# Delta-rule attention with an MLP: transposes in 128x128 blocks, one Gram matmul for K and Q, and a scheduler that models instruction fetch

## The chip, the cores and the metric

The kernel runs on one core of a Trainium2 chip. The metric is the device time of one execution in microseconds (us). A run over 1.5% above the fastest of its kernel counts as slow. All ratios and the medians of the experiments are of fast runs alone; all profiles are of fast runs. TensorE is called PE in the profile, its weight loads PEld (each matmul first loads its stationary operand); VectorE is DVE, ScalarE ACT, GpSimd POOL. An engine waits for another by a semaphore, a counter that the other one raises.

## The reference, cut to what matters

```python
# q, k, v: (4, 8, 768, 48); beta: (4, 8, 768)
k_n = k / (np.linalg.norm(k, axis=-1, keepdims=True) + 1e-06)
for t in range(S):
    y[:, :, t] = q_t @ state
    v_old = state^T @ k_n_t
    state = state + beta_t * outer(k_n_t, v_t - v_old)
# then, on x = y with heads joined: (3072, 384)
h = x @ w_in                 # 384 -> 2048
out = gelu_tanh(h) @ w_out   # 2048 -> 384
```

The recurrence is done in 12 chunks of 64 tokens for 32 heads (16 pairs). Within a chunk a 64x64 triangular system is solved for every head, by a Newton iteration on small matmuls. Only the state passes from chunk to chunk. The MLP runs on tiles of one or two finished chunks, so its matmuls can be laid between the small ones of later chunks.

## The kernel before: the parts that matter

The program is built as a list of some 1040 operations. A list scheduler in the kernel file orders them, with modelled durations, a table of priorities found by search (`OFFSET`), and a tolerance for waiting (`NEAR`). An operation on TensorE is a batch of matmuls. The file has no model of how instructions reach an engine.

```python
UNITS = [[0]] + [[c, c + 1] for c in range(1, NCH - 1, 2)] + [[NCH - 1]]

# Gram: K K^T and K Q^T of a chunk, separately; 4 quadrants of the array, 64 columns each
for o in range(2):
    def gd(h=h, o=o):
        for m in range(p0 // 2, p1 // 2):
            for (hh, a) in ((0, 0), (1, 1), (0, 1), (1, 0)):
                ...
                r.append((bank(h, hh)[cc, mo:mo + C], KQT[i][rr, 0, m, cc], KQT[i][rr, o, m, cc], True, True, True))
    # ... (cut: one DVE multiply of 1024 columns for W, one for DT)

# transposes of W for the Newton iteration: every 64x64 block, to both row halves
def tr_w(t):
    for p in range(n):
        for o in range(2):
            for a in range(2):
                ins = t.transpose(xb(o)[rows(a ^ o), p, :], W[rows(a), p, :], identB[rows(a), :])
```

## Time and profile before

| | before |
|---|---|
| median of 3 runs | 327.86 us (326.28 to 331.25, the last one slow) |
| profiled span | 324.9 us |
| matmuls, each with a weight load | 7998 |
| TensorE, VectorE, ScalarE, GpSimd busy | 76%, 53%, 52%, 37% |
| instruction packets | 63 |

From the page of the kernel before: busy time and number of instructions of each engine, and one of the DMA queues (packets, MB, share of the 16 DMA engines):

```profile
span 324.9 us, 16859 instructions
PE 247.8 (76%) x7998; PEld 163.1 (50%) x7998; DVE 173.7 (53%) x227; ACT 169.8 (52%) x255; POOL 120.3 (37%) x80
...
q8 instruction: 63, 1.03, 1.3%
```

63 packets of 16 KB: 1.03 MB. Matmuls and weight loads are 15,996 instructions, and 15,996 / 256 = 62.5. So this queue carries TensorE's program, 256 instructions to a packet. Such a packet is called a block below, and the place where one ends and the next begins a border.

From the table of waits of the kernel before (who waited for what: us in total, times, longest):

```profile
PEld ps L342 <- issue: 58.8, 80, 3.9
...
PE ps L342 <- issue: 35.4, 34, 3.4
```

"issue" is a wait for nothing that the profile shows. PE and PEld overlap, so the two rows count many of the same gaps twice; they are not to be read as 94 us of lost time.

From the chain of waits of the kernel before, 195 to 225 us (start, length, what):

```profile
196.24 0.91 issue
197.16 2.98 PE ps L342 x103
200.14 0.57 issue
200.71 3.28 PE ps L342 x115
203.99 3.38 issue
207.37 8.33 PE ps L342 x215
...
218.76 0.66 issue
219.42 3.75 PE ps L342 x128
223.17 0.90 issue
```

The reader should see a rhythm: about 120 matmuls (some 250 instructions), a gap without a releaser, and again. Counted in TensorE's own instruction order, the gaps lie exactly 256 apart.

From the groups of instructions of the kernel before, the two that the change rewrites (busy us, mean ns, idle before):

```profile
L342 PE MATMUL ps<-KQT 48*64 48x64 bf16 x768 | 13.5, 215 | 5.3 <-issue 2.7 <-ACT KQT L335 1.1 <-DMA KQT<-KQ 1.0
...
L687 PE MATMUL ps<-identB,Wi 64*64 64x64 bf16 x768 | 11.8, 210 | 10.4 <-issue 7.3 <-DVE Wi L326 2.0 <-DVE F_0 L326 0.9
```

And the end of its chain of waits. From 282.69 us on there are only MLP matmuls:

```profile
282.69 29.37 PE ps L342 x178
...
312.70 8.31 PE ps L342 x51
```

### The profile page before, as it was taken

What the parts mean: (1) busy time and instruction counts of PE and PEld (TensorE: products, weight loads), DVE (VectorE), ACT (ScalarE), POOL (GpSimd) and SP (SyncE); (2) the same over time, 40 slices, a digit from 0 to 9 for tenths busy, and PEclk for the clock granted to TensorE, in tenths of its full rate; (3) what the DMA queues carried; (4) which work ended last, traced back from release to release, by engine and by line L of the source; (5) the groups of instructions that cost most, each with busy time, mean ns of one, the idle gap of its engine ahead of it and who ended that gap; (6) DMA issues with size and microseconds to landing.
All of it is one profiled execution on the core that took longest, in us unless ns stands there. A gap on an engine that the chain in (4) does not pass through costs nothing.

```text
span 324.9 us, 16859 instructions
## 1 busy us (share of the span) xinstructions
PE 247.8 (76%) x7998; PEld 163.1 (50%) x7998; DVE 173.7 (53%) x227; ACT 169.8 (52%) x255; POOL 120.3 (37%) x80
## 2 busy tenths in 40 slices
PE   1176445548977786897788988598899888999995
PEld 1155344536754444554455555454466555555652
DVE  3489856546665743876774564366747454210021
ACT  2555334547475356665675745165755586428220
POOL 5747805224961744698373102265500000000000
PEclk9999999999998999999999999899999999999999
DMA  6997997994215984397800087537200102110012
GB/s 123 180 215 127 163 164 135 162 143 75 52 27 110 135 173 91 69 168 136 185 28 4 18 129 136 80 78 118 52 28 28 52 6 43 36 48 26 24 50 73
DMA packets 108757, 29.99 MB, mean 92 GB/s; under 512 B 103184, under 2 KB 108304, under 8 KB 108688
## 3 DMA queue, kind: packets, MB, share of 16 engines
q1 hardware_dynamic: 106144, 25.77, 43.7%
q0 software_dynamic: 2544, 3.15, 5.8%
q8 instruction: 63, 1.03, 1.3%
q14 instruction: 6, 0.05, 0.0%
HBM read 20.64 MB, written 4.72 MB: 78 GB/s over the span
## 4 chain that ended last, share of the span: by engine, by line
PE 65%; issue 13%; DMA 12%; SPq 4%; ACT 3%; DVE 2%
PE ps L342 63%; DMA qf<-in_q_dram 8%; SPq L350 4%; DMA kf<-in_k_dram 2%; DMA KQT<-KQ 2%; PE ps L687 2%; ACT Z_0 L335 1%; DVE F_0 L326 1%; ACT gT L335 1%; ACT Z_1 L335 1%; ACT x L335 0%; ACT L335 0%; PE ps L865 0%; DVE osb L331 0%; DVE S L326 0%
## 5 line engine op out<-in xcount | busy, mean ns | idle before, releaser
L335 ACT ACTIVATE gT<-ps 128x512 bf16<-128x512 f32 (+1 forms) x112 | 57.5, 538 | 51.0 <-PE ps L342 49.1
L342 PE MATMUL ps<-xT,W 128*128 128x512 bf16 (+1 forms) x336 | 78.0, 361 | 2.0 <-issue 2.0
L342 PE MATMUL ps<-W,gT 128*128 128x384 bf16 x384 | 69.5, 329 | 0.3 <-DVE osb L331 0.3
L326 DVE TENSOR_TENSOR F_1<-twoI,ps 128x1024 bf16<-128x1024 bf16 (+4 forms) x35 | 32.3, 928 | 28.9 <-PE ps L342 28.8
L342 PEld LDWEIGHTS ps<-W,gT 128*128 128x128 bf16 x384 | 35.7, 98 | 23.3 <-DVE osb L331 0.6
L326 DVE TENSOR_TENSOR F_0<-twoI,ps 128x1024 bf16<-128x1024 bf16 (+4 forms) x35 | 32.4, 929 | 27.5 <-PE ps L342 27.1
L342 PEld LDWEIGHTS ps<-xT,W 128*128 128x128 bf16 x336 | 28.7, 100 | 24.0 <-issue 2.6
L326 POOL TENSOR_TENSOR Wi<-Wi,identB 128x1024 bf16<-128x1024 bf16 (+1 forms) x10 | 19.3, 1930 | 44.4 <-DVE Wi L326 38.8
L326 POOL TENSOR_TENSOR KQ<-kf,rn 128x768 bf16<-128x768 f32 (+1 forms) x12 | 17.4, 1450 | 48.5 <-PE ps L342 30.5
L331 DVE COPY osb<-ps 128x384 f32<-128x384 f32 x20 | 11.1, 555 | 42.5 <-PE ps L342 42.3
L335 ACT ACTIVATE Z_1<-ps 128x1024 bf16<-128x1024 f32 (+1 forms) x23 | 20.4, 893 | 23.3 <-PE ps L342 23.1
L335 ACT ACTIVATE Z_0<-ps 128x1024 bf16<-128x1024 f32 (+2 forms) x26 | 20.9, 808 | 21.8 <-PE ps L342 21.6
L326 POOL TENSOR_TENSOR sr<-ss,half 128x16 f32<-128x16 f32 x9 | 26.2, 2916 | 9.7 <-DVE ss L564 9.7
L342 PE MATMUL ps<-Z_1,F_1 64*64 64x64 bf16 (+1 forms) x672 | 21.5, 207 | 8.5 <-issue 7.4
L342 PE MATMUL ps<-X,Z_1 64*64 64x64 bf16 (+2 forms) x672 | 19.4, 200 | 9.6 <-issue 6.7
L342 PEld LDWEIGHTS ps<-Z_1,F_1 64*64 64x64 bf16 x672 | 18.3, 119 | 16.0 <-issue 12.0
L342 PE MATMUL ps<-X,Z_0 64*64 64x64 bf16 (+2 forms) x672 | 22.4, 206 | 4.1 <-ACT Z_0 L335 3.0
L326 POOL TENSOR_TENSOR NU<-mU,bcol 128x1024 f32<-128x1024 f32 x12 | 23.7, 1972 | 1.6 <-DVE Wi L326 1.0
L342 PEld LDWEIGHTS ps<-X,Z_1 64*64 64x64 bf16 x672 | 16.1, 119 | 16.1 <-issue 10.3
L342 PE MATMUL ps<-Z_0,F_0 64*64 64x64 bf16 (+1 forms) x672 | 21.9, 210 | 2.0 <-issue 2.0
L342 PEld LDWEIGHTS ps<-X,Z_0 64*64 64x64 bf16 x672 | 19.2, 124 | 4.4 <-ACT Z_0 L335 3.2
L335 ACT ACTIVATE x<-ps 64x768 bf16<-64x768 f32 x24 | 19.3, 803 | 2.9 <-PE ps L342 2.4
(86 smaller groups left out, 387.9 us busy)
## 6 DMA issues: line engine op xcount, KB each, us to landing
qf<-in_q_dram SPq DMA_DIRECT2D x24, 192.0 KB, 4.3
kf<-in_k_dram SPq DMA_DIRECT2D x24, 192.0 KB, 4.1
vf<-in_v_dram SPq DMA_DIRECT2D x48, 96.0 KB, 3.1
out_dram<-osb SPq DMA_DIRECT2D x20, 192.0 KB, 1.9
W<-in_moe_w_in_dram POOLq DMA_DIRECT2D x3, 512.0 KB, 6.5
W<-in_moe_w_out_dram POOLq DMA_DIRECT2D x4, 384.0 KB, 8.0
out_dram<-osb SPq DMA_DIRECT2D x8, 96.0 KB, 2.5
BL<-in_beta_dram SPq DMA_DIRECT2D x2, 96.0 KB, 2.3
```

Of the source, the lines that this page charges most:

```text
L326: return lambda e: e.tensor_tensor(out() if callable(out) else out, a() if callable(a) else a, b() if callable(b) else b, op)
L331: return lambda e: e.tensor_copy(out, a() if callable(a) else a)
L335: return lambda e: e.activation(out, a() if callable(a) else a, func)
L342: ins = t.matmul(out, lhsT, rhs, start=st, stop=sp_, skip_group_check=skip)
L350: return lambda e: e.dma_start(out, a)
L687: ins = t.transpose(xb(o)[rows(a ^ o), p, :], W[rows(a), p, :], identB[rows(a), :])
```

## The change

The intent: fewer TensorE instructions for the same arithmetic, and an order made in the knowledge that instructions arrive in blocks. The diff, cut to its core:

```diff
-NEAR = {"pe": 0.081, "dve": 0.32, "act": 0.006, "pool": 0.0, "sp": 0.0}
+NEAR = {"pe": 0.231, "dve": 0.371, "act": 0.068, "pool": 0.0, "sp": 0.0}
+BLOCK, FETCH = 256, ((75.0, 4.7), (1e9, 3.8))
     # ... OFFSET: every priority replaced (cut)
+class Fetch:      # a border every BLOCK instructions opens FETCH us after the last one at the earliest
+    def run(self, t, d, n): ...
...
-                    late = max(0.0, t - free_at[e])
+                    stall = fetch.peek(t, pe_cost(o, t), o.n) if e == "pe" else 0.0
+                    late = max(0.0, t + stall - free_at[e])
...
-    UNITS = [[0]] + [[c, c + 1] for c in range(1, NCH - 1, 2)] + [[NCH - 1]]
+    UNITS = [[0], [1], [2], [3, 4], [5, 6], [7, 8], [9, 10], [11]]
...
-            for o in range(2):                       # gram: K K^T, then K Q^T
-                            r.append((bank(h, hh)[cc, mo:mo + C], KQT[i][rr, 0, m, cc], KQT[i][rr, o, m, cc], ...))
+            for g in range(p0 // 8, p1 // 8):        # gram: K [K Q]^T, half of the heads each
+                            r.append((bank(h, hh)[cc, 128 * mm:128 * mm + 128], KQT[i][rr, 0, m, cc], KQT[i][rr, :, m, cc], ...))
...
             def tr_w(t):
-                for p in range(n):
-                    for o in range(2):
-                        for a in range(2):
-                            ins = t.transpose(xb(o)[rows(a ^ o), p, :], W[rows(a), p, :], identB[rows(a), :])
+                for m in range(n // 2):
+                    ins = t.transpose(xb(0)[:, 2 * m:2 * m + 2, :]..., W[:, 2 * m:2 * m + 2, :]..., identG[:, :])
+                for m in range(n // 2 - 1):
+                    ins = t.transpose(xb(1)[:, 2 * m:2 * m + 2, :]..., W[:, 2 * m + 1:2 * m + 3, :]..., identG[:, :])
+                for r, p in ((0, n - 1), (1, 0)):
+                    ins = t.transpose(xb(1)[rows(r), n - 2:n, :]..., W[:, p, :], identG[:, :])
```

The Newton iteration's index into the transposed blocks follows the new layout (cut). Also cut: the costs given to the scheduler, and the transposes' choice of PSUM banks (the accumulators that TensorE writes), six instead of eight.

More of the change, by code (lines that the diff above doesn't have):

```diff
@@ L18 @@
 BURST = 0.0
-BANKS = {"t": (0, 6), "s": (0, 8), "f": (6, 8), "l": (0, 8), "i": (0, 8)}
+BANKS = {"t": (0, 6), "s": (0, 8), "f": (6, 8), "l": (0, 8), "i": (0, 6)}
 FULL = ("f", "l", "i")
-NEAR = {"pe": 0.081, "dve": 0.32, "act": 0.006, "pool": 0.0, "sp": 0.0}
+BLOCK, FETCH = 256, ((75.0, 4.7), (1e9, 3.8))
 LOW_CLOCK = 57.0
 OFFSET = {
-    "pe:DT": -35.0, "KQT>": 104.0, "mU": 25.3, "twoI>": -18.0, "R>": 7.8, "xT": 47.7,
-    "DT>": 9.6, "pe:x": -14.7, "none": 5.5, "sr": 169.6, "Zc": -59.6, "idI>": -14.2,
-    "mU>": -132.1, "X>": -71.5, "Wi>": -35.3, "pe:KQ": -27.3, "xT>": -18.3, "vf": -50.8,
-    "pe:xT!": -11.4, "ss>": -23.1, "kf": -13.2, "pe:Zc": -90.8, "KQz>": -68.5, "BL": -53.2,
-    "osb>": 71.4, "identG>": -199.6, "gT": 80.7, "identB>": -67.3, "pe:BL!": -63.5, "x": 12.4,
-    "pe:Za": -65.3, "F>": -31.8, "identF": -45.1, "Za>": -11.5, "KQT": 58.6, "W": -17.7,
-    "pe:KQT": -29.7, "S>": -138.3, "half>": -39.5, "pe:gT!": -0.3, "sq": -103.5, "KQq": -96.7,
-    "R": -67.0, "Za": 21.1, "Wi": 31.4, "KQ": 50.9, "bcol>": -30.9, "KQ>": 30.8,
-    "U>": -4.6, "KQx": -54.1, "rn>": -6.8, "NU": 24.7, "Fi": -16.0, "qf": -46.0,
-    "pe:Wi": -36.4,
+    "KQ>": -8.9, "W": -121.8, "pe:KQT": -54.1, "osb>": -30.4, "gT": -91.7, "identB>": 138.8,
+    "U>": -80.5, "mU>": 13.4, "pe:x": -98.8, "twoI>": 43.7, "idI>": -49.6, "sr": 35.2,
+    "xT>": 34.8, "KQz>": -33.8, "sq": -79.4, "identG>": 59.4, "mU": -25.4, "pe:BL!": -160.3,
+    "X>": -54.3, "bcol>": -80.4, "pe:KQ": -50.3, "KQT": 16.4, "Fi": -60.4, "KQ": -223.4,
+    "KQq": 26.8, "NU": -71.5, "KQx": -79.9, "S>": 29.3, "xT": 125.0, "none": 128.0,
+    "Za>": 10.0, "pe:gT!": -23.5, "R>": 76.7, "rn>": 7.5, "vf": 25.8, "KQT>": -193.0,
+    "half>": -155.1, "Zc": -6.3, "pe:Wi": 13.4, "identF": -115.4, "kf": -32.8, "x": -31.9,
+    "Wi": -40.4, "BL": -7.9, "F>": -60.6, "pe:Zc": 20.9, "qf": 83.2, "pe:Za": -18.7,
+    "ss>": 8.3, "R": -107.5, "Za": -11.9, "Wi>": -42.6, "DT>": -63.2, "pe:xT!": -20.2,
+    "pe:DT": -64.7,
 }
+NEAR = {"pe": 0.231, "dve": 0.371, "act": 0.068, "pool": 0.0, "sp": 0.0}
 class Op:
     __slots__ = ("idx", "cost", "fns", "deps", "prio", "alloc", "uses", "dma", "lat",
-                 "eng", "start", "end", "count", "clock", "sync", "mode", "bw", "hard", "kind")
+                 "eng", "start", "end", "count", "clock", "sync", "mode", "bw", "hard", "kind", "n")
 def kind_of(o, reads, writes):
@@ L48, in kind_of, with __init__, peek, run @@
     return stem(x if isinstance(x, str) else "ps") + (">" if "dve" in o.cost else "")
+class Fetch:
+    def __init__(self):
+        self.n, self.last = 0, -10.0
+    def peek(self, t, d, n):
+        n0, last = self.n, self.last
+        end = self.run(t, d, n)
+        self.n, self.last = n0, last
+        return end - t - d
+    def run(self, t, d, n):
+        late = 0.0
+        k = self.n // BLOCK + 1
+        while n and k * BLOCK < self.n + n:
+            at = t + d * (k * BLOCK - self.n) / n + late
+            wait = max(0.0, self.last + next(f for x, f in FETCH if at < x) - at)
+            late += wait
+            self.last = at + wait
+            k += 1
+        self.n += n
+        return t + d + late
 class Plan:
@@ L69, in op @@
         o.cost, o.fns, o.prio, o.dma, o.lat, o.mode, o.bw, o.hard = cost, fns, prio, dma, lat, mode, bw, hard
+        o.n = 0
+        if isinstance(cost.get("pe"), tuple):
+            o.cost = dict(cost, pe=cost["pe"][0])
+            o.n = 2 * cost["pe"][1] + 1
         o.alloc = tuple(alloc)
@@ L124, in schedule @@
         prio = [o.prio + OFFSET.get(o.kind, 0.0) for o in ops]
+        fetch = Fetch()
         def pe_cost(o, t):
@@ L207, in schedule @@
                 burst0 = t
-            o.eng, o.start, o.end = e, t, t + (pe_cost(o, t) if e == "pe" else o.cost[e])
+            o.eng, o.start, o.end = e, t, fetch.run(t, pe_cost(o, t), o.n) if e == "pe" else t + o.cost[e]
             if o.dma:
@@ L385, in bass_deltanet__then__act_gelu_tanh_kernel @@
     FC = FF // 128
-    TILES = [[0]] + [[c, c + 1] for c in range(1, NCH - 1, 2)] + [[NCH - 1]]
-    UNITS = [[0]] + [[c, c + 1] for c in range(1, NCH - 1, 2)] + [[NCH - 1]]
+    TILES = [[0], [1, 2], [3, 4], [5, 6], [7, 8], [9, 10], [11]]
+    UNITS = [[0], [1], [2], [3, 4], [5, 6], [7, 8], [9, 10], [11]]
     NT = len(TILES)
@@ L541, in bt_mms @@
                      True, True, True) for t in range(3)]
-        op({"pe": 1.0}, {"pe": f_mms(bt_mms)}, mode="f", reads=["BL0", "BL1", "identF"], writes=[hb_ + (0,), hb_ + (1,)], alloc=[(hb_, 1)], prio=-50)
+        op({"pe": (1.0, 3)}, {"pe": f_mms(bt_mms)}, mode="f", reads=["BL0", "BL1", "identF"], writes=[hb_ + (0,), hb_ + (1,)], alloc=[(hb_, 1)], prio=-50)
         for a in range(2):
@@ L605, in trk @@
                     return ins
-                op({"pe": 0.55}, {"pe": trk}, mode="i", reads=(kq[:2] if g == 0 else kq) + ["identG"], writes=[ht], alloc=[(ht, 1)], prio=pr + 0.2)
+                op({"pe": (0.55, 8)}, {"pe": trk}, mode="i", reads=(kq[:2] if g == 0 else kq) + ["identG"], writes=[ht], alloc=[(ht, 1)], prio=pr + 0.2)
                 dst = KQT[i][:, :, 4 * g:4 * g + 4, :]
@@ L618, in mm_pe @@
             t = max(31.0, cols / 2.4 + 3.0) / tiles
-            return {"pe": 1e-3 * n_ins * max(8.3, t)}
+            return {"pe": (1e-3 * n_ins * max(8.3, t), n_ins)}
         def md(c):
@@ L647, in pv, with gd @@
                 return t.rearrange("q (m h) t -> q m h t", h=2)
-            for o in range(2):
+            for g in range(p0 // 8, p1 // 8):
                 h = handle()
-                def gd(h=h, o=o):
+                gs = slice(8 * g, 8 * g + 8)
+                def gd(h=h, g=g):
                     r = []
-                    for m in range(p0 // 2, p1 // 2):
+                    for mm in range(4):
+                        m = 4 * g + mm
                         for (hh, a) in ((0, 0), (1, 1), (0, 1), (1, 0)):
-                            rr, cc, mo = slice(64 * hh, 64 * hh + D), rows(a), C * (m - p0 // 2)
-                            r.append((bank(h, hh)[cc, mo:mo + C], KQT[i][rr, 0, m, cc], KQT[i][rr, o, m, cc], True, True, True))
-                    return r
-                def gv(h=h):
-                    return banks2(h)[:, :, 0:C * n // 2].rearrange("q h (m t) -> q m h t", t=C)
-                op(mm_pe(2 * n, C, 4), {"pe": f_mms(gd)}, mode=md(c), reads=KTn, writes=[h], alloc=[(h, 2)], prio=pr + o)
-                if o == 0:
-                    op(d_ps(C * n), {"dve": f_tt(pv(W), gv, pv(NU[j2][:, ps_, :]), ALU.mult)},
-                       reads=[h, f"NU{j2}"], writes=Wn, prio=pr + 0.1)
-                else:
-                    op(d_ps(C * n), {"dve": f_tt(pv(DTb[i][:, ps_, :]), gv, mU[:, :].unsqueeze(1).unsqueeze(1).to_broadcast(
-                        [128, n // 2, 2, C]), ALU.mult)}, reads=[h] + MASKU, writes=nms("DT", i, p0, p1), prio=pr + o + 0.1)
@@ new lines, in gd, with gv @@
+                            rr, cc = slice(64 * hh, 64 * hh + D), rows(a)
+                            r.append((bank(h, hh)[cc, 128 * mm:128 * mm + 128], KQT[i][rr, 0, m, cc], KQT[i][rr, :, m, cc], True, True, True))
+                    return r
+                def gv(o, h=h):
+                    return lambda: banks2(h).rearrange("q h (m k t) -> q m h k t", k=2, t=C)[:, :, :, o, :]
+                op(mm_pe(16, 128, 4), {"pe": f_mms(gd)}, mode=md(c), reads=[f"KQT{i}{g}"], writes=[h], alloc=[(h, 2)], prio=pr + g * 0.5)
@@ L669, in intra_in @@
+                op(d_ps(512), {"dve": f_tt(pv(Wb[j2][:, gs, :]), gv(0), pv(NU[j2][:, gs, :]), ALU.mult)},
+                   reads=[h, f"NU{j2}"], writes=[f"Wi{j2}_{8 * g}"], prio=pr + g * 0.5 + 0.1)
+                op(d_ps(512), {"dve": f_tt(pv(DTb[i][:, gs, :]), gv(1), mU[:, :].unsqueeze(1).unsqueeze(1).to_broadcast(
+                    [128, 4, 2, C]), ALU.mult)}, reads=[h] + MASKU, writes=[f"DT{i}_{8 * g}"], prio=pr + g * 0.5 + 0.4)
             for x, t, a_, b_, alu, rd in (("W", W, W, identB, ALU.add, Wn + ["identB"]), ("Z", Z, twoI, W, ALU.subtract, Wn + ["twoI"])):
@@ L683, in tr_w @@
                 ins = None
-                for p in range(n):
-                    for o in range(2):
-                        for a in range(2):
-                            ins = t.transpose(xb(o)[rows(a ^ o), p, :], W[rows(a), p, :], identB[rows(a), :])
+                for m in range(n // 2):
+                    ins = t.transpose(xb(0)[:, 2 * m:2 * m + 2, :].rearrange("q p t -> q (p t)"),
+                                      W[:, 2 * m:2 * m + 2, :].rearrange("q p t -> q (p t)"), identG[:, :])
+                for m in range(n // 2 - 1):
+                    ins = t.transpose(xb(1)[:, 2 * m:2 * m + 2, :].rearrange("q p t -> q (p t)"),
+                                      W[:, 2 * m + 1:2 * m + 3, :].rearrange("q p t -> q (p t)"), identG[:, :])
+                for r, p in ((0, n - 1), (1, 0)):
+                    ins = t.transpose(xb(1)[rows(r), n - 2:n, :].rearrange("q p t -> q (p t)"), W[:, p, :], identG[:, :])
                 return ins
-            op(mm_pe(4 * n, 64, 4), {"pe": tr_w}, mode=md(c), reads=Wn + ["identB"], writes=hx, alloc=[(hx[0], 1), (hx[1], 1)],
+            op({"pe": (0.058 * (n + 1), n + 1)}, {"pe": tr_w}, mode="i", reads=Wn + ["identG"], writes=hx, alloc=[(hx[0], 1), (hx[1], 1)],
                prio=pr + 0.4)
@@ L742, in body @@
                             b_, q_ = (p % 2, p // 2) if byh else (p // per, p % per)
-                            late = j == 4 and p % 2
+                            flips, n = (p % 2 if j == 4 else j % 2), lhs.shape[1]
                             for a in range(2):
-                                r_ = rows(a)
+                                r_, o = rows(a), a ^ (p % 2)
                                 fl = is_z and (j < 3 or (j == 3 and p % 2 == 0))
-                                rh = rhs[r_, p, lo:hi] if is_z else rhs[r_, (1 - j % 2 if late else j % 2), p, lo:hi]
+                                xp = 2 * (p // 2 if o == 0 else (p - 1) % n // 2) + (a ^ flips)
+                                rh = rhs[r_, p, lo:hi] if is_z else rhs[r_, o, xp, lo:hi]
                                 w = hi - lo
@@ L866, in trx @@
                     return ins
-                op({"pe": 0.45}, {"pe": trx}, mode="i", reads=xr + ["identB"], writes=[hx], alloc=[(hx, 1)], prio=pr - 2000)
+                op({"pe": (0.45, 12)}, {"pe": trx}, mode="i", reads=xr + ["identB"], writes=[hx], alloc=[(hx, 1)], prio=pr - 2000)
                 op({"act": 0.82, "dve": 0.55}, {"act": f_act(xT[:, s, :, 0:64], xb), "dve": f_cp(xT[:, s, :, 0:64], xb)},
@@ L878, in m1 @@
                              kt == KT - 1, False) for kt in range(KT)]
-                op({"pe": 1e-3 * KT * (w / 2.4 + 4)}, {"pe": f_mms(m1)}, mode=mo, reads=[f"xT{s}"] + W1N, writes=[h],
+                op({"pe": (1e-3 * KT * (w / 2.4 + 4), KT)}, {"pe": f_mms(m1)}, mode=mo, reads=[f"xT{s}"] + W1N, writes=[h],
                    alloc=[(h, 1)], prio=pr + fc * 2.4)
@@ L888, in m2 @@
                                  fc == FC - 1, False) for fc in range(8 * part, 8 * part + 8)]
-                    op({"pe": 1.31}, {"pe": f_mms(m2)}, mode=mo,
+                    op({"pe": (1.31, 8)}, {"pe": f_mms(m2)}, mode=mo,
                        reads=[f"gT{(FC * t + fc) % NGS}" for fc in range(8 * part, 8 * part + 8)] + W2N + ([h] if part else []),
@@ L918, in bass_deltanet__then__act_gelu_tanh_kernel @@
             newton(u)
-            if n_ + 1 < len(UNITS) and n_ > 0:
+            if n_ + 1 < len(UNITS):
                 for c in UNITS[n_ + 1]:
+                    if c < 3:
+                        continue
                     prep(c)
```

## The prediction

> **What bounds the kernel now.** Not arithmetic. The page gives TensorE 76% busy, VectorE 53%, ScalarE 52%, GpSimd 37%. In the table of waits, weight loads wait for "issue" 58.8 us in 80 places and matmuls 35.4 us in 34, that is, for nothing the profile shows. In the order of TensorE's instructions these gaps sit 256 apart (the 1217th, 1729th, 1985th, 2241st, 2497th ...). The DMA queue of kind "instruction" moved 63 packets of 16 KB, and 15,996 matmuls and weight loads are 62.5 times 256: the packets are TensorE's program. The Trainium skill, "Runtime: NRT & Kernel Launch", section "Instruction fetch mechanics", says instructions come in 16 KiB blocks of 256, which this trace confirms; it also says the fetch is hidden behind issue, which this trace contradicts: the gaps at block borders sum to about 51 us.
>
> The rhythm: after a border the next packet starts about 1.1 us later, and the border after it opens about 2.4 us after that. So borders cannot be closer than 3.3 to 3.8 us (4 to 5.5 us before 75 us, where loads fill the DMA engines). Small matmuls start about 8.5 ns apart late in the run, so a block of 128 takes 1.1 us. From 75 to 283 us the kernel crosses 51 borders in 208 us, 4.08 us each: within a tenth of the fetch limit. After 283 us only MLP matmuls are left (163 and 216 ns each); that tail of 42 us is TensorE work.
>
> **What the change does.**
> - Gram: 64 matmuls a chunk become 32 of twice the columns: 384 fewer in all.
> - Transposes: 64 a chunk become 17 (18 for a chunk alone): 560 fewer. Today 64 take about 0.6 us; 17 of 128 columns at about 54 ns (a quarter of the 512-column 216 ns) are an estimated 0.9 us: a loss of about 4 us in sum.
> - So 944 of 7998 matmuls go, with weight loads 1888 instructions, 7.4 blocks.
> - VectorE: gram evictions in halves, an estimated 3 us more; off the path.
> - The schedule knows of the fetch: it should put MLP matmuls into blocks that would stall. Chunk 1 no longer waits for chunk 2's loads.
>
> **On the critical path.** Nearly all removed blocks outside the tail count, since the border rhythm is the path. From 75 us on: 5.5 blocks of 3.8 to 4.1 us, 21 to 23 us. Before: 1.9 blocks of 4.7 us, at most 9 us, partly swallowed by the input loads (12% of the chain of waits is DMA); I count 5. Better interleaving: the periods could come from 4.08 to about 3.9 us, some 5 us. Against it: 4 us of transposes, and switches between 64x64 and 128x128 tiles. The tail stays. 328 - 22 - 5 - 5 + 0 to 4: about 296 us; I put 295, range 283 to 308. Chances: faster by over 2% 0.94, within 2% 0.04, slower 0.02.
>
> **What would show it.** 55 or 56 instruction packets; 7054 matmuls; the spacing of packets in the middle still 3.5 to 4 us; issue waits falling from 94 us over both rows to about 60; small matmuls finished near 255 us instead of 283; tail near 40 us; transposes about 0.9 us a chunk.
>
> **What would make it wrong.** Semaphore round trips of the Newton chain (0.3 us at many waits) or evictions becoming the limit; a longer MLP tail because less MLP fits in the shorter middle; drains around 128x128 transposes; a start bound by loads alone; a tuned order that fits its model better than the chip.

## The result, and the profile after

The changed kernel takes 305.29 us, median of 4 (304.36 to 305.81), beside 327.07 us for the two fast ones of the kernel before's four runs (median of all four 329.56 us). The ratio is 0.9331, 95% interval 0.9275 to 0.9387. A ratio here is the mean time of one kernel's fast runs over that of the other's of the same rounds, so not quite the ratio of the medians. The prediction was 295 us with a range of 283 to 308: the direction and the range held, the gain was 22 us instead of 33.

From the page of the changed kernel:

```profile
span 304.1 us, 15009 instructions
PE 249.4 (82%) x7054; PEld 162.1 (53%) x7054; DVE 173.0 (57%) x264; ACT 168.5 (55%) x266; POOL 120.0 (39%) x80
...
q8 instruction: 55, 0.90, 1.2%
```

7054 matmuls and 55 packets, as forecast. TensorE's busy time did not fall: 247.8 us became 249.4 although the run is 21 us shorter. The Trainium skill, "Perfetto Trace Analysis", section "Identifying the Most-Contended Engine", says that matmul busy time is no good measure of how close TensorE is to its limit, and names the share of weight loads beside the share of peak arithmetic instead. The share of weight loads rose from 50% to 53% only because the span shrank (163.1 us against 162.1): it shows that there was room, not what filled it.

From its table of waits:

```profile
PEld ps L374 <- issue: 35.5, 52, 6.2
...
PE ps L374 <- issue: 11.7, 10, 3.1
```

From its chain of waits, 195 to 225 us:

```profile
194.92 7.00 PE ps L374 x233
201.92 0.55 PE ps L718 x8
202.47 0.39 PE ps L721 x7
...
203.03 7.35 PE ps L374 x233
...
210.43 2.63 PE ps L374 x102
...
213.13 8.31 PE ps L374 x225
```

In the same stretch of time, where the kernel before had five gaps of 0.57 to 3.38 us on its chain, the changed one has none over 0.1 us on its own. L718 to L724 are the new transposes, 17 for a chunk in about 1.1 us.

From its groups of instructions, the rewritten ones:

```profile
L374 PE MATMUL ps<-KQT 48*64 48x128 bf16 x384 | 12.1, 253 | 10.4 <-issue 5.3 <-DMA KQT<-KQ 3.3 <-ACT x L367 1.5
...
L718 PE MATMUL ps<-identG,Wi 128*128 128x128 bf16 x96 | 9.5, 242 | 3.4 <-DVE Wi L358 3.1 <-issue 0.3
L721 PE MATMUL ps<-identG,Wi 128*128 128x128 bf16 x80 | 8.3, 241 | 0.0
L724 PE MATMUL ps<-identG,Wi 128*64 128x128 bf16 x32 | 4.3, 265 | 0.0
```

768 Gram matmuls became 384, 768 transposes became 208. A mean duration is a latency, not a rate: the starts of the new transposes lie about 65 ns apart and those of the old 9.3 ns, so 17 x 65 = 1.1 us replace 64 x 9.3 = 0.6 us. The Gram takes about 32 x 13.9 = 0.44 us a chunk where it took 64 x 9.4 = 0.60 us; these two means depend on where long intervals are cut off. In array time the change is thus a small loss, 12 x (0.5 - 0.16) = 4 us, an estimate.

And the end of its chain of waits:

```profile
271.43 28.80 PE ps L374 x180
```

**Where the time went.** Every interval between two successive starts on TensorE was put into one class: after an MLP matmul; ending at an instruction that waits for a semaphore; ending at a block border without such a wait and over 0.15 us long ("border gaps"); the rest, which is the small matmuls. The classes add up to the span. An interval can fit two classes, and another way of sorting them moves some us from one column to another; the border gaps and the differences between the two kernels stay within about 1 us.

| us | MLP | small matmuls | border gaps | semaphore waits | sum |
|---|---|---|---|---|---|
| before | 115.8 | 90.6 | 51.5 (42 gaps) | 66.6 | 324.5 |
| after | 118.2 | 93.9 | 15.8 (17 gaps) | 75.8 | 303.7 |

35.7 us of border gaps went. 9.2 us came back as semaphore waits, 3.3 us as small matmuls (the transposes) and 2.4 us as MLP.

The same by stage. The first stage ends when the MLP of chunks 3 and 4 starts, the second with the last chunk's matmuls on DT.

| us | first stage | second stage | MLP tail |
|---|---|---|---|
| before | 145.6 | 133.8 | 45.5 |
| after | 149.9 | 119.0 | 35.2 |

By this cut the first stage gained nothing: it is 4 us longer, and all the time came off the second stage (14.8 us) and the tail (10.3 us). But the stages do not hold the same work. In the first stage the changed kernel runs 192 MLP matmuls, the kernel before 152; in the tail it has 186 left of 248. The first stage's own border gaps fell from 28.0 to 11.0 us; against that stand about 7 us for the 40 MLP matmuls moved ahead, 9.6 us more of semaphore waits (43.1 to 52.7) and 4.4 us of small matmuls. From here the questions were: is it the number of instructions or the new order that pays, and why does the first stage get nothing?

### The profile page after: what moved, and what is told of

The parts are those of the page before. It is cut to its first block, busy times and chain, and to the rows that moved or that the text cites. A ratio compares the mean times of both kernels' runs of the same rounds, so it can differ in the third digit from the quotient of the medians.

```text
span 304.1 us, 15009 instructions
## 1 busy us (share of the span) xinstructions
PE 249.4 (82%) x7054; PEld 162.1 (53%) x7054; DVE 173.0 (57%) x264; ACT 168.5 (55%) x266; POOL 120.0 (39%) x80
## 2 busy tenths in 40 slices
DMA packets 108749, 29.86 MB, mean 98 GB/s; under 512 B 103184, under 2 KB 108304, under 8 KB 108688
## 3 DMA queue, kind: packets, MB, share of 16 engines
q1 hardware_dynamic: 106144, 25.77, 45.5%
## 4 chain that ended last, share of the span: by engine, by line
PE 63%; DMA 14%; DVE 6%; ACT 5%; issue 5%; SPq 3%; POOL 2%
PE ps L374 57%; DMA KQT<-KQ 5%; DMA qf<-in_q_dram 5%; DMA kf<-in_k_dram 3%; SPq L382 3%; PE ps L718 2%; DVE F L358 2%; ACT Z L367 2%; PE ps L721 1%; PE ps L636 1%; DVE Wi L358 1%; ACT x L367 1%; POOL KQ L358 1%; DVE DT L358 1%; ACT KQ L367 1%
## 5 line engine op out<-in xcount | busy, mean ns | idle before, releaser
L367 ACT ACTIVATE Z<-ps 128x512 bf16<-128x512 f32 (+2 forms) x80 | 59.0, 746 | 45.5 <-PE ps L374 44.5
L358 DVE TENSOR_TENSOR F<-twoI,ps 128x512 bf16<-128x512 bf16 (+4 forms) x80 | 65.7, 830 | 32.4 <-PE ps L374 31.6
L374 PE MATMUL ps<-W,gT 128*128 128x384 bf16 x384 | 68.4, 327 | 0.0
L374 PE MATMUL ps<-Z,F 64*64 64x64 bf16 (+1 forms) x1920 | 54.9, 200 | 15.2 <-ACT X L367 6.1
L374 PEld LDWEIGHTS ps<-Z,F 64*64 64x64 bf16 x1920 | 46.5, 114 | 27.0 <-issue 11.4
L374 PE MATMUL ps<-X,Z 64*64 64x64 bf16 (+2 forms) x1920 | 54.8, 198 | 6.5 <-ACT Z L367 2.1
L374 PEld LDWEIGHTS ps<-X,Z 64*64 64x64 bf16 x1920 | 47.1, 116 | 15.4 <-issue 6.4
L358 DVE TENSOR_TENSOR Wi<-ps,NU 128x512 bf16<-128x512 f32 x24 | 16.5, 687 | 11.4 <-PE ps L374 11.4
L374 PE MATMUL ps<-KQT 48*64 48x128 bf16 x384 | 12.1, 253 | 10.4 <-issue 5.3
L358 POOL TENSOR_TENSOR Z<-twoI,Wi 128x1024 bf16<-128x1024 bf16 (+1 forms) x10 | 19.3, 1930 | 0.2
L367 ACT ACTIVATE X<-ps 128x512 bf16<-128x512 bf16 (+1 forms) x17 | 13.4, 796 | 7.6 <-PE ps L724 7.1
```

Source lines behind the costliest of these rows:

```text
L358: return lambda e: e.tensor_tensor(out() if callable(out) else out, a() if callable(a) else a, b() if callable(b) else b, op)
L367: return lambda e: e.activation(out, a() if callable(a) else a, func)
L374: ins = t.matmul(out, lhsT, rhs, start=st, stop=sp_, skip_group_check=skip)
```

## The experiments

Two theories. COUNT: the gain is the 7.4 blocks that need not be fetched. ORDER: the gain is the fetch-aware order, which fills the blocks with MLP work. The experiments ran on other chips of the same kind, where the kernel before took 329.5 to 331.7 us, so I compare ratios to the kernel before of the same call. A point is 1% of the time before, about 3.3 us; the changed kernel stands at 0.9331, a gain of 6.7 points. Twelve kernels ran; all but r8 gave the right result.

### r1: the changed kernel's order, the old number of instructions

```diff
-   r.append((bank(h, hh)[cc, 128 * mm:128 * mm + 128], KQT[i][rr, 0, m, cc], KQT[i][rr, :, m, cc], ...))
+   for o in range(2):
+       r.append((bank(h, hh)[cc, 128 * mm + C * o:128 * mm + C * o + C], KQT[i][rr, 0, m, cc], KQT[i][rr, o, m, cc], ...))
    # and tr_w with its layout as before; costs given to the scheduler unchanged
```

The scheduled order and the PSUM banks are identical to those of the changed kernel (compared entry by entry); only what each operation emits differs.

> The changed kernel in exactly its own order of operations, but each gram matmul issued as two of 64 columns and the transposes in 64x64 blocks as before: 7998 matmuls again, 63 instruction packets, results right. Theory COUNT (the gain is the 7.4 blocks that are no longer fetched, each worth its border period): 305 + 7.4 x 3.8 us - 4 us for the cheaper transposes, about 325 to 330 us. Theory ORDER (the gain is the fetch-aware order, which leaves slack at the borders: mean spacing about 4.2 us where 3.6 would do): 303 to 312 us, with border gaps growing from 15 us to 25 at most.

Measured: 327.36 us, ratio 0.985 (0.9729 to 0.9972). Of 6.7 points, 5.2 are gone, 17 us, with an uncertainty of about 1.3 points. COUNT holds; the border gaps rose well past the 25 us that ORDER allowed (below). From the page of this run:

```profile
PE 254.8 (78%) x7998; PEld 164.5 (50%) x7998; DVE 172.2 (53%) x264; ACT 168.7 (52%) x266; POOL 119.9 (37%) x80
...
q8 instruction: 63, 1.03, 1.3%
```

From its chain of waits, 195 to 225 us:

```profile
198.12 7.97 PE ps L374 x249
206.09 1.35 issue
...
208.24 1.91 PE ps L374 x55
210.15 1.56 issue
211.71 4.21 PE ps L374 x123
215.92 0.65 issue
```

The rhythm of the kernel before is back. Its border gaps are 37.1 us (after: 15.8), its semaphore waits unchanged at 74.9 us. The array time it saves, 4 us, has to be added to see the price of the blocks: (17 + 4) / 7.4 = 2.9 us for each, an estimate from these numbers, less than the 3.8 I had assumed. Some 4 us of it may belong to the clock (see "The clock").

### r2: the old order, only the new transposes

```diff
     def tr_w(t):
-        (64 blocks of 64x64)
+        (17 or 18 blocks of 128x128, new layout), cost and mode for the scheduler unchanged
```

> The kernel before in exactly its own order, only the inverse's transposes in 128x128 blocks: 7438 matmuls, 58 or 59 packets. COUNT: 4.4 blocks x 4 us saved, 4 to 5 us of slower transposes given back: about 314 to 317 us. ORDER: within 2% of before, 324 to 331 us.

Measured: 320.99 us, ratio 0.969 (0.955 to 0.9831): 10 us less, with the order of the kernel before untouched and about 6 us more array time (12 x 0.5). (10 + 6) / 4.4 = 3.6 us a block, an estimate. From its page:

```profile
PE 253.2 (79%) x7436; PEld 167.0 (52%) x7436; DVE 170.2 (53%) x227; ACT 170.0 (53%) x255; POOL 120.6 (38%) x80
...
q8 instruction: 58, 0.95, 1.2%
```

The median lies 4 us above COUNT's range, because this chip was slower (331.7 us for the kernel before, not 327.07); the ratio times 327.07 us is 317 us, the upper end of the range. The gain is clear of noise and COUNT holds, at a lower price than the 4 us expected. ORDER expected less than 2%; the interval just reaches that, so r2 alone does not exclude it.

### r3: new forms, old scheduler

```diff
     (before, with the new Gram and transposes; scheduler, OFFSET, NEAR and UNITS of before)
```

> Both new forms (7054 matmuls, 55 packets), scheduler, priorities and units of before. COUNT: nearly all of the gain, 300 to 308 us. ORDER: little of it, 318 to 328 us.

Measured: 322.16 us, ratio 0.971 (0.9589 to 0.9831). This is what ORDER expected, not COUNT. The stages show why: first 149.9, second 116.2, tail 51.8 us. The attention part ends at 266 us, even earlier than in the changed kernel (269 us), but the MLP has been left to the end. 274 MLP matmuls lie in its tail, against 248 before and 186 in the changed kernel. So fewer instructions shorten the recurrence, and this order, made without knowing of the borders, fails to bring the MLP along.

### r4: old forms, fetch model added

```diff
     (changed scheduler, UNITS and forms of before, OFFSET and NEAR of before)
```

> Old forms (7998 matmuls, 63 packets), priorities and units of before, only the fetch model added to the scheduler. COUNT: no gain, 322 to 332 us. ORDER: much of the gain, 308 to 316 us, with border gaps of 51 us falling below 35.

Measured: 335.85 us, ratio 1.0131 (1.0026 to 1.0236). ORDER's gain is absent. The border gaps fell to 40.3 us, the semaphore waits grew to 80.9 us. With priorities searched for the other model this is only a weak test; r9 is the fair one.

### r5 and r6: each half of the instruction count alone, in the changed kernel's order

r5 has the Gram split and the new transposes kept; r6 has the transposes split and the new Gram kept. The edits are the two halves of r1.

> The changed kernel in its own order, only each gram matmul issued as two of 64 columns: 7438 matmuls, 58 or 59 packets, about 2 us more array time. COUNT: 3 blocks at the 3.5 us that run r1 gives a block, 2 us of array time: about 316 to 318 us. Rival SLACK (borders of the changed kernel lie wider apart than the fetch needs, so the first added blocks are hidden and only the whole 7.4 hurt): 304 to 309 us.

> The changed kernel in its own order, only the transposes in 64x64 blocks again: 7614 matmuls, 59 or 60 packets, about 5 us less array time. COUNT: 4.4 blocks at 3.5 us less 5 us: about 314 to 317 us. SLACK: 301 to 308 us.

Measured: r5 315.56 us, ratio 0.9554 (0.9477 to 0.963), 58 packets; r6 313.60 us, ratio 0.9529 (0.9467 to 0.9591), 60 packets. They lose 2.2 and 2.0 points, together 4.2 beside r1's 5.2: within the uncertainty the halves add up. SLACK, which expected the first blocks to be hidden, is refuted: the border gaps rose from 15.8 us to about 26 (r5) and 31 (r6). The size of the loss is less sure, since part of it may be the clock's (see "The clock"). The transposes buy 4.4 blocks with slower array time, the Gram only 3 with faster, and they are worth about the same.

### r7: the changed kernel's scheduler without its fetch times

```diff
-BLOCK, FETCH = 256, ((75.0, 4.7), (1e9, 3.8))
+BLOCK, FETCH = 256, ((75.0, 0.0), (1e9, 0.0))
```

> The changed kernel with the fetch times in the scheduler set to zero, so it orders without knowing of the fetch; priorities, units and forms as changed; 55 packets. If the fetch model itself makes the order good (theory MODEL): 315 to 325 us with border gaps near 30 us, as with the old scheduler in run r3. If it is the re-tuned priorities and units (theory TUNING): 303 to 309 us.

Measured: 324.95 us, ratio 0.9854 (0.9796 to 0.9912): 5.2 points lost with all 55 packets and the same priorities. The border gaps are 27.0 us. The stages are 160.4, 107.9 and 54.9 us: as in r3 the middle is short, and MLP is left to the tail (289 matmuls). MODEL holds for this set of priorities. The loss lies in the tail (20 us) and the first stage (10 us); the middle gives 11 back.

### r8: cheaper loads of q, k and v (wrong)

```diff
-   parts = [(t[s][64 * a:64 * a + 64, :, :], sv[a, C * c:C * c + C, :, :])]      # 1024 pieces of 192 bytes
+   parts = [(t[s][64 * a:64 * a + 64, :, :].rearrange(...), flat[row0:row0 + 64, :])]  # 64 rows of 3072 bytes
```

> The changed kernel with the loads of q, k and v taken as whole rows of 3072 or 1536 bytes instead of pieces of 192 bytes: same bytes, far fewer descriptors, same order; the result is wrong on purpose. If the first 150 us, where the change gained nothing, are held by the input loads and by their pressure on the fetch (theory LOADS): 288 to 298 us, chunk 3 done 8 us or more earlier than at 129 us, border spacing before 75 us below 5 us. If the Newton chain and its evictions hold them: 302 to 306 us.

Measured: 298.05 us, ratio 0.9059 (0.9008 to 0.9109), 2.7 points or 9 us below the changed kernel. The Trainium skill, "DMA: Bandwidth & Descriptors", section "Specifications", gives 512 bytes as the smallest transfer at line rate; the pieces here have 192. The trace agrees in direction: packets under 512 bytes fell from 103,184 to 29,456, and the loads got cheaper. By stretches (PE, PEld, DVE, ACT and POOL busy us, granted clock, DMA share, GB/s), the changed kernel:

```profile
0.00:75.00 75.00, 42.21 (x1225) 32.81 (x1225) 48.27 (x97) 36.09 (x63) 37.74 (x37) 0.82 0.85 145
```

and r8:

```profile
0.00:75.00 75.00, 46.29 (x1362) 35.62 (x1363) 52.33 (x103) 38.76 (x68) 43.24 (x40) 0.77 0.71 158
```

137 more matmuls are done by 75 us, with more bytes moved in a smaller share of the DMA engines. Chunk 0 is done at 45.8 us instead of 51.0, chunk 3 at 122.8 instead of 129.4 (6.6 us, where I had asked for 8). The semaphore waits fell from 75.8 to 65.2 us, and in the first stage from 52.7 to 43.1, what the kernel before has there; the border gaps stayed (15.7 us), and the border spacing before 75 us did not fall below 5 us. So the loads hold the start through waits for data, not through their pressure on the fetch: that half of my expectation was wrong.

### r9: old forms with the same care

```diff
     (forms of before; changed scheduler and UNITS; OFFSET and NEAR searched anew, about 4000 trials by the scheduler's own time)
```

> Old forms (7998 matmuls, 63 packets) with the fetch model, the new units and priorities searched anew for these forms against the scheduler's own time (4000 trials), so that old forms get the same care as the new. If the instruction count is worth what runs r1, r5 and r6 say even under an order made for it (COUNT): 317 to 325 us. If the new order alone could have given the gain with the old forms (ORDER): 304 to 311 us.

Measured: 323.65 us, ratio 0.9786 (0.9725 to 0.9847), border gaps 40.4 us. The old forms under an order searched for them gain 2.1 points of 6.7.

### r10, r11 and r12: units, later weights, and a control

r10 puts chunks 1 and 2 into one unit again, r11 asks for the output weights later; both with priorities searched anew. r12 is the changed kernel with its priorities searched a little further: 0.2% better by the scheduler's own time.

> New forms, fetch model, priorities searched anew, but chunks 1 and 2 in one unit as before. If running chunks 1 and 2 apart is worth something: 309 to 314 us. If it is not: 303 to 307 us.

> New forms and scheduler, but the output weights (3 MB) are asked for after chunk 4's keys instead of after chunk 0's values, priorities searched anew. If the weights' transfer delays chunks 1 to 3 (LOADS): 296 to 302 us, chunk 3 done before 125 us. If not: 304 to 310 us.

> Control: the changed kernel with priorities moved by a further search, the scheduler's own time 0.2% shorter. It shows how far two orders differ on the chip that the scheduler takes for equal: 301 to 308 us if the scheduler's time is a good guide; a larger distance is the size that differences between searched orders must exceed to mean anything.

Measured: r10 314.34 us, ratio 0.953 (0.9469 to 0.9591); r11 309.98 us, ratio 0.9365 (0.9295 to 0.9435); r12 314.86 us, ratio 0.9509 (0.943 to 0.9588). The control decides how to read them: an order that the scheduler takes for equal is 1.8 points slower on the chip. It is one such order only; another could lie further off. So r10's loss of 2.0 points says nothing about the units, and r11's loss of 0.3 nothing about the weights. It also limits r3, r4, r7 and r9, which all have other orders: r7's 5.2 and r3's 3.8 points exceed 1.8, r9's 4.5 points behind the changed kernel do too, but their sizes are good to some two points only. r1, r2, r5 and r6 keep an order exactly and don't suffer from this. No version here beat the changed kernel with a right result.

## Why the prediction was right or wrong

**The bound: right.** I said that the borders between instruction blocks are the path. r2 removes 560 matmuls in an unchanged order, makes the array slower, and gains 3.1 points. r1, r5 and r6 put instructions back and lose 5.2, 2.2 and 2.0. The forecast packets (55), matmuls (7054) and the missing gain in array time were right too, the last a little low: 1.1 us a chunk for the transposes, not 0.9.

**The price of a block: mis-sized.** The step was "5.5 blocks of 3.8 to 4.1 us, 21 to 23 us" after 75 us, plus 5 us before. For all 7.4 blocks together that is 27 us. r1 shows 17 us net, 2.9 us a block with the array time added. The step before it, "borders cannot be closer than 3.3 to 3.8 us", was a little too strong as well: the closest pair lies 3.07 us apart in the kernel before and 2.87 in the changed one. Part of a block's period is work that must be done anyway: in the changed kernel from 81.6 to 257.4 us the borders are 4.29 us apart (41 periods), further than the fetch needs, and only 17 of some 54 borders still show a gap, where 42 of 62 did. A removed block then takes away its gap, not its period: r1's border gaps are 21.3 us longer than the changed kernel's, again 2.9 us for each of 7.4 blocks.

**"The periods could come from 4.08 to about 3.9 us, some 5 us": wrong.** They grew to 4.29 us, because more MLP work was put into them: before the tail there are 534 MLP matmuls for 54 borders, where there were 472 for 61. What the order buys shows where I said "the tail stays": the tail fell from 45.5 to 35.2 us. r3 and r7, with the same 55 packets and orders blind to the fetch, have tails of 51.8 and 54.9 us. The two parts of the change help each other: count in the new order is worth 5.2 points, the fetch model with the new count also about 5 (r7), but the new order with the old count only 1.5 (r1), and the new count in the old scheduler 2.9 (r3). Apart they make 4.4 points, together 6.7; that the difference, 2.3, is more than the scatter between orders is not shown.

**The start: the largest miss.** I counted on 5 us gained before 75 us; the whole first stage came out 4 us longer. It is not that the borders were dear there, for 17 us of its border gaps went: the time was filled by MLP work moved ahead and by waits. Chunk 2 is done at 97.1 us instead of 101.2, chunk 4 at 139.2 instead of 137.2. r1 splits it, by one profile of each: with the old count the new order needs 165.2 us for the first stage, where the kernel before needs 145.6. So the new order lengthens the first stage by about 20 us, and the smaller count gives 15 of them back. Of the 20, some 10 are the MLP matmuls moved ahead (partly at half clock) and 10 are longer semaphore waits (53.1 us against 43.1). r1's later stages are shorter than before (126.0 and 35.2 us against 133.8 and 45.5), so the order trades the start for the end and by itself gains only 1.5 points, 5 us (0.3 to 2.7 points). I had named "a start bound by loads alone" as a risk, and r8 shows that the start of the changed kernel is held by loads for 6 us of the first stage (143.6 against 149.9). A piece of its chain of waits shows the kind of wait:

```profile
62.83 1.49 POOL KQ L358
...
64.33 4.95 DMA KQT<-KQ
...
69.57 1.38 issue
```

Chunk 3's normalised keys come late, then their transposing DMA takes 5 us, then a border. I had also warned of semaphore waits: they grew by 9 us, nearly all of it in the first stage, and r8 takes as much away there, which points to the loads.

**Luck.** The total stayed in the range because misses cancelled. Of 27 us for blocks 17 came; the 5 us for better interleaving came in size (r1's 1.5 points), but not by shorter periods; the tail, which was to stay, gave 10 us, and the first stage none. Other marks missed too: the small matmuls ended at 269 us and not near 255, and VectorE's 3 us more did not come (173.7 to 173.0 us). The waits for "issue" fell further than I said, to 47 us and not 60.

**Left open.** Which part of the new order makes the waits of the start longer (chunks 1 and 2 apart, the priorities, the tolerance for waiting) was not settled: r10 and r11 drown in the scatter between orders. Whether cheap loads would help the kernel before as much as the changed one was not run.

**The clock.** The page of the changed kernel prints a lower mean granted clock, 0.937 against 0.989, which could be taken for the cause of its slow start. The matmuls themselves say otherwise. The Trainium skill, "TensorE: Matmul & The Clock Gate", part 1, gives 106.7 ns from start to start for 128 columns with the array cold (half clock) and 55.6 ns warm. The traces have both: 107 ns for the first transposes of both kernels and 56 ns for later ones of the changed kernel. In the kernel before the array is cold wherever this can be measured up to about 84 us (14.8 to 30.3 and 68.4 to 84.6 us), although the page prints full speed there; its first clock record is at 85.6 us. From its timeline (start, length of the three matmuls together):

```profile
78.44 0.82 PE L342 MATMUL ps<-xT,W 128*128 128x256 bf16 x3
...
88.60 0.50 PE L342 MATMUL ps<-xT,W 128*128 128x256 bf16 x3
```

The changed kernel's records begin at 33.9 us and show 38 us at half clock before 110 us. Its first transposes, from 12.4 us on, are cold as well. So both start cold, and the two means can't be compared. What the clock costs can be counted at the MLP matmuls: those that start about twice as far apart as usual, without a wait or a border between, cost 2.1 us more than at full speed in the kernel before (20 of them) and 2.3 us in the changed one (22). So the clock does not explain the gain. In runs that slow the changed kernel it does take a part: 6.1 us in r1 (48 matmuls), 5.5 in r5, 6.2 in r6 and 5.5 in r7, some 3 to 4 us more than in the changed kernel, about one point each. In the other direction r2 has 2.8 us, little more than the kernel before. These are single profiles; whether the added border gaps made the array slower there, or chance, is not shown. If chance, a block costs (17 + 4 - 4) / 7.4 = 2.3 us by r1, and r5 and r6 lose about one point each. The border gaps by themselves still rose: from 15.8 us to 37.1 in r1, about 26 in r5 and 31 in r6.

## What to carry to other kernels

Where an engine has thousands of short instructions, divide its instruction count by the block size and look for gaps at that distance: they have no releaser in the profile, and they are paid in instructions, not in array time, so a form that is slower in the array but has fewer instructions can win. More of the gain is kept if long matmuls are spread over the blocks that would otherwise stall; where they were not (r3, r7), a part moved into a tail. A stage that got no shorter may hold more work: count it before saying that nothing was gained. To judge a part of such a change, keep the order exactly and change only what is emitted: two orders that a scheduler takes for equal differed by 1.8% on the chip.

## What the Trainium skill lacked or had wrong

- "Runtime: NRT & Kernel Launch", section "Instruction fetch mechanics": blocks of 256 instructions are confirmed (63 packets for 15,996 instructions), but the page has the fetch hidden by the pace of issue, and here it is not hidden: 42 gaps at borders, 51.5 us of a 324.9 us span, and 7.4 blocks put back cost 17 us net (r1).
- The same page gives no rate for the fetch. In the kernel before the next packet mostly started 1.0 to 1.3 us after a crossed border where the borders followed closely, and a border opened at the earliest 2.2 us after its packet's start; the packets themselves took about 0.9 to 1.4 us.
- "TensorE: Matmul & The Clock Gate", part 1, warns that clock records can be unreliable. Here the trap is a plain one that no page names: before its first record (85.6 us in the kernel before, 33.9 us in the changed one) the page of the profile prints full clock, while matmuls 107 ns apart instead of 56 show half.
- "Perfetto Trace Analysis", section "Identifying the Most-Contended Engine": its measures for TensorE say how much room there is, not where it goes. Here the time of weight loads (163.1 and 162.1 us) and of matmuls (247.8 and 249.4 us) stayed while the span fell by 21 us; the waits for "issue" showed it (58.8 and 35.4 us, then 35.5 and 11.7). No page says that a fetch stall looks like a wait without a releaser.
